# Second stage of a two-MLP kernel: additions and weight conversions held in program order; retention loads and one transpose reordered

## The chip, the cores and the metric

The kernel runs on one core of one Trainium2 chip, as one program. The metric is the device time of an execution in microseconds. The time before is 562.62 us, the median of three runs (562.59 to 562.89). One more execution was profiled; its own time and span are in the table below. Engines are named as the profile names them: PE is TensorE, DVE is VectorE, ACT is ScalarE, POOL is GpSimd, SP is the engine whose queue issues most of the DMAs.

## The reference

Three pieces run one after the other. Retention (linear attention with decay) works on 2 batches of 8 heads, 768 positions and head size 64, here in blocks:

```python
intra = (q_b @ k_b.T * Dmask) @ v_b
inter = (q_b * lam_pow) @ kv_state
out_b = intra + inter
kv_state = lam_block * kv_state + (k_b * rev_pow).T @ v_b
```

Its output, laid out as 1536 tokens by 512, goes through two MLPs of width 2048: `y = relu(x @ w_in)**2 @ w_out`, then `z = leaky(y @ w2_in) @ w2_out` with leaky(h) = max(0.01 h, h). The weights arrive as 64-bit floats. The output is 32-bit.

## The kernel before, in words

**Retention.** The work is cut into 12 units of 128 positions, numbered 0 to 11. Unit i needs its k, q and v (256 KB each, loaded by SP at L65). PE transposes k and q (L279), ACT copies the transposes out of PSUM (L283, L287), PE multiplies them into scores (L300), DVE masks the scores with powers of the decay (L305), PE forms the state update from v and the decayed k (L331) and the output (L360, L362). The loop over i runs one unit ahead in parts: pass i does scores and mask of unit i+1, transposes of unit i+2, then state and output of unit i. Loads run two passes ahead of their use: pass i loads k and q of unit i+4 and v of unit i+2, and pass i+2 uses all three, in the order k, q, v. Three weight pieces are loaded in between. In this part the order on PE and SP is the order of the code.

**The two MLPs.** Each MLP runs in four stages over 512 of the 2048 hidden columns; stage (0, 0) is the first, stage (0, 1) the second. Every matmul is done as three matmuls on operands split into a high and a low part (`three`, L549 to L551). From the second stage on, the first layer treats token tiles 0 and 1 together, as a *pair* (`first_pair`), with seven products of 2 by 2 blocks in place of eight. For each half h = 0, 1 of the stage's columns the products go into four PSUM banks A, B, C, D: A (A11·B11), B (S2·T2), D (A22·T4), B again (S3·T3, added onto the same bank), C (S1·T1), A again (A12·B21), C again (S4·B22). One product is six matmuls of 128x512. Between them DVE makes sums (`plus`, L621), with s1 the copy of A:

- s2 = B + s1, which must have read B before the second B product is added onto it
- r22 = B + s1 with the full B, then s1 = D + r22, which is hidden block 1 of its half for token tile 0
- r22 = C + r22, which must have read C before the second C product is added onto it
- s2 = C + s2 with the full C

`put` sends each finished block through `activate`: in the second stage ACT does relu (L487), the square into the high part (L488, tile g0h or g1h) and the square in place (L489), then DVE subtracts to the low part (L493, tile g0l or g1l). The blocks of token tile 0, h by block, are: block 1 from s1, block 0 from A. The second layer (`second`) starts with g0h and g0l of token tile 0.

**Weight conversion.** Each 64-bit weight piece (tile raw) is turned into float parts by a row of DVE steps (L145, L146, L148, L151 on tile hb) behind one ACT step (L142); for the next stage's pair, sums of weight blocks follow (L446 to L451, tiles rb and sw) and a low part (L169). `convert` issues one such step at each `yield` of PE's work that does not say False. L151 frees the raw tile, so that SP may issue the next weight load.

**What sets the order.** PE, and in retention SP too, run in code order. For DVE, ACT and POOL the tile scheduler chooses the order in each engine's queue from priorities (`plus` and `put` run with a raised priority), except for steps given to `keep_in_program_order`. Once built, each engine works through its queue in order: an instruction that waits holds up all that are behind it.

Of the kernel before, what the change touches and what calls it, by code (L numbers as in the profile page):

```python
# [15 lines left out]
ALU = mybir.AluOpType  # L16
# [4 lines left out]
def tile_retention_then_two_mlps(  # L21
# [39 lines left out]
    def plain():  # L61
        return fp.tile([P, TT], F32, tag="f", name="f")

    def dma(dst, src):
        return nc.sync.dma_start(dst, src)  # L65
# [7 lines left out]
    def source(l, s, n, h):  # L73
        w = ((w1, w2), (w3, w4))[l][n]
        if n == 0:
            return w[:, s * FS + h * CW:s * FS + (h + 1) * CW].rearrange("(k p) f -> p k f", p=P)
        return w[s * FS + h * CW:s * FS + (h + 1) * CW, :].rearrange("(k p) f -> p k f", p=P)

    order = [(0, 0, 0, 0), (0, 0, 0, 1), (0, 0, 1, 0), (0, 0, 1, 1)]
    stages = [(l, s) for l in range(2) for s in range(NS)]  # L80
# [10 lines left out]
    def fetch():  # L91
        if todo:
            key = todo.pop(0)
            r = raw.tile([P, 4 * CW], I64, tag="raw", name="raw")
            k = 4 if key[2] == 0 else 2
            dma(r.rearrange("p (k f) -> p k f", k=k), source(*key))
            fetched.append((key, r))
# [80 lines left out]
    def convert(pin=False):  # L178
        for piece in list(at_work):
            step = next(piece[1], False)  # L180
            if step is False:
                at_work.remove(piece)
            elif step is not None:
                if pin:
                    tc.keep_in_program_order(step)
                return
        if fetched and len(at_work) < 2:
            begin(pin)
# [18 lines left out]
    def retention(ctx_att, att):  # L207
# [10 lines left out]
        def load(i, name):  # L218
            b, c = units[i]
            t = nat[name].tile([P, H, D], F32, tag=name, name=name)  # L220
            dma(t, {"q": q, "k": k, "v": v}[name][b, :, c * C:(c + 1) * C, :].rearrange("h p d -> p h d"))
            nats[i, name] = t

        ve = nc.vector
# [40 lines left out]
        def transposes(i, names="kq"):  # L265
            early = i < 4
            if names[0] == "k":
                both = tr.tile([P, 2, NP, 2, D], F32, tag="kq", name="kqT", bufs=2)
                kT[i], qT[i] = (both[:, n] for n in range(2))
            for name in names:  # L270
                n, dst = ((0, kT), (1, qT))[name == "q"]
                if early:
                    ps = [bank()[:, 0:NP * D].rearrange("p (a s) -> p a s", a=NP) for _ in halves]
                elif n == 0:
                    two = [bank().rearrange("p (n a s) -> p n a s", n=2, a=NP) for _ in halves]
                src = nats[i, name]
                for p in range(NP):
                    for half, r in enumerate(halves):
                        nc.tensor.transpose(ps[half][:, p] if early else two[half][:, n, p],  # L279
                                            src[r, 2 * p:2 * p + 2, :].rearrange("s h d -> s (h d)"), ident[r, r])  # L280
                if early:
                    for half in range(2):
                        nc.scalar.copy(dst[i][:, :, half], ps[half])  # L283
                    dst[i] = dst[i].rearrange("p a f s -> p a (f s)")
            if not early:
                for half in range(2):
                    nc.scalar.copy(both[:, :, :, half], two[half])  # L287
                kT[i], qT[i] = (both[:, n].rearrange("p a f s -> p a (f s)") for n in range(2))
# [81 lines left out]
        n_units = len(units)  # L370
# [15 lines left out]
        mask(0)  # L386
        scale_q(1)
        for i in range(n_units):
            if i + 4 < n_units:
                load(i + 4, "k")  # L390
                load(i + 4, "q")
            if i + 2 < n_units:
                load(i + 2, "v")
            if i == 3:
                next(piece)
            if i == 9:
                next(piece)
                fetch()
                fetch()
            if i + 1 < n_units:  # L400
                scores(i + 1)
                mask(i + 1)
            if i == 1:
                state(i)
                output(i, range(2))
            if i + 2 < n_units:
                transposes(i + 2)
                scale_q(i + 2)
            if i == 1:
                output(i, range(2, NP))  # L410
            else:
                state(i)
                output(i)
            if i + 1 < n_units:
                scale_k(i + 1)
            for _ in range({5: 1, 6: 2, 7: 1, 8: 1, 11: 2}.get(i, 0)):
                convert(pin=True)
# [160 lines left out]
    def first_pair(l, s):  # L578
        last = (l, s) == stages[-1]
        new_g(l, s, 0)  # L580
        new_g(l, s, 1)
        ve = nc.vector
        w = {}
        for h in range(2):
            hi, lo = wts[l, s, 0, h]
            for i in range(2):
                for j in range(2):
                    w[h, f"A{i + 1}{j + 1}"] = [x[:, 2 * j:2 * j + 2, i * P:(i + 1) * P] for x in (hi, lo)]
            for n in range(4):
                w[h, f"S{n + 1}"] = [sums[l, s, 0, h][:, part, n] for part in range(2)]  # L590
        x = {
            "B11": (xhi[0][:, 0:2], xlo[0][:, 0:2]),
            "B21": (xhi[0][:, 2:4], xlo[0][:, 2:4]),
            "B22": (xhi[1][:, 2:4], xlo[1][:, 2:4]),
            "T1": (xhi[1][:, 0:2], xlo[1][:, 0:2]),
        }
        for n in (2, 3, 4):
            x[f"T{n}"] = (tt[n][:, 0], tt[n][:, 1])
        ps, s1, s2, r22 = {}, {}, {}, {}

        def product(h, where, a, b, start=True):
            if start:
                ps[h, where] = bank()
            (ah, al), (bh, bl) = w[h, a], x[b]
            ops = []
            for j in range(2):
                ops += [(ah[:, j], bh[:, j]), (ah[:, j], bl[:, j]), (al[:, j], bh[:, j])]
            three(ps[h, where], ops, start, True, not start)
            return ps[h, where]

        def put(h, src, r, i, t):
            m = 2 * h + i
            with tc.high_priority(offset=400 if t == 0 else 0):
                if last:
                    activate_last(t, m, src)
                else:
                    activate(l, src, r, g[t][0][:, m], g[t][1][:, m], src is r and (l, s) != stages[1])

        def plus(h, out, where, other):
            with tc.high_priority(offset=400):  # L620
                ve.tensor_tensor(out=out, in0=ps[h, where], in1=other, op=ALU.add)  # L621

        both = range(2)
        for h in both:
            b = product(h, "A", "A11", "B11")
            s1[h] = plain()
            nc.scalar.copy(s1[h], b)
            yield True
        for h in both:
            product(h, "B", "S2", "T2")  # L630
            s2[h] = plain()
            plus(h, s2[h], "B", s1[h])
            yield True
        for h in both:
            product(h, "D", "A22", "T4")
            yield (l, s) != stages[1]
        if last:
            opened.add(("sums", l, s))
        for h in both:
            product(h, "B", "S3", "T3", False)  # L640
            r22[h] = plain()
            plus(h, r22[h], "B", s1[h])
            plus(h, s1[h], "D", r22[h])
            put(h, s1[h], s1[h], 1, 0)
            yield last
        for h in both:
            product(h, "C", "S1", "T1")
            plus(h, r22[h], "C", r22[h])
            yield (l, s) != stages[1]
        for h in both:  # L650
            put(h, product(h, "A", "A12", "B21", False), plain(), 0, 0)
            yield last
        for h in both:
            product(h, "C", "S4", "B22", False)
            plus(h, s2[h], "C", s2[h])
            yield last
        for h in both:
            put(h, r22[h], r22[h], 1, 1)
            put(h, s2[h], s2[h], 0, 1)
        if last:  # L660
            sums_last(0)
            sums_last(1)
# [162 lines left out]
    with tc.manual_schedule(engines={mybir.EngineType.PE}):  # L825
        for l, s in stages:
            for part in stage(l, s):
                for room in part:
                    if room is not False:
                        convert()  # L830


# [23 lines left out]
```

## Time and profile before

| what | value |
|---|---|
| time, median of three runs | 562.62 us |
| the profiled execution's own time | 563.24 us |
| its span on the core | 561.5 us |
| PE busy | 551.3 us (98%) |
| DVE busy | 413.5 us (74%) |
| ACT busy | 296.2 us (53%) |
| stretch 0 to 54 us: PE, DMA share | 49.41 us busy, 0.95 |
| stretch 60 to 120 us: PE, DVE | 60.00 us and 59.04 us busy |
| stretch 120 to 160 us: PE, DVE | 37.94 us and 30.37 us busy |

The span is the time between the first and the last instruction on the core; 1.74 us of the execution lie around it. Retention fills the first 54 us. The first stage runs from there to 119.45 us and the second stage's pair starts there. A busy share says only that an engine had something to do; which wait ended last in a place is read from the views of waits and of time order.

### The profile page before, as it was taken

What the parts mean: (1) busy time and instruction counts of PE and PEld (TensorE: products, weight loads), DVE (VectorE), ACT (ScalarE), POOL (GpSimd) and SP (SyncE); (2) the same over time, 40 slices, a digit from 0 to 9 for tenths busy, and PEclk for the clock granted to TensorE, in tenths of its full rate; (3) what the DMA queues carried; (4) which work ended last, traced back from release to release, by engine and by line L of the source; (5) the groups of instructions that cost most, each with busy time, mean ns of one, the idle gap of its engine ahead of it and who ended that gap; (6) DMA issues with size and microseconds to landing.
All of it is one profiled execution on the core that took longest, in us unless ns stands there. A gap on an engine that the chain in (4) does not pass through costs nothing.

```text
span 561.5 us, 8346 instructions
## 1 busy us (share of the span) xinstructions
PE 551.3 (98%) x3245; PEld 465.5 (83%) x3245; DVE 413.5 (74%) x603; ACT 296.2 (53%) x470; POOL 87.6 (16%) x99
## 2 busy tenths in 40 slices
PE   7999999999999999999999999999999999999997
PEld 6989888887788888888888888888888888888897
DVE  5668999999662895639989996549472774629877
ACT  3444898555782456553366576445462375436520
POOL 4855000000203101220000000000213011310131
PEclk9999999999999999999999999999999999999999
DMA  8998255454619516584413233533729423560534
GB/s 201 213 229 264 76 166 190 169 159 141 129 25 245 123 12 142 150 150 138 144 56 114 75 97 128 176 124 109 118 84 182 111 23 52 75 76 1 163 139 149
DMA packets 68055, 71.84 MB, mean 128 GB/s; under 512 B 39856, under 2 KB 43952, under 8 KB 68016
## 3 DMA queue, kind: packets, MB, share of 16 engines
q1 hardware_dynamic: 60960, 58.60, 34.0%
q0 software_dynamic: 6912, 12.59, 15.9%
q8 instruction: 25, 0.41, 0.3%
q10 hardware_dynamic: 144, 0.13, 0.1%
q14 instruction: 14, 0.11, 0.1%
HBM read 49.29 MB, written 22.02 MB: 127 GB/s over the span
## 4 chain that ended last, share of the span: by engine, by line
PE 82%; DVE 8%; DMA 6%; ACT 2%; issue 1%; SPq 0%; ACTq 0%
PE ps L551 75%; DMA raw<-in_moe_w_in 2%; PE ps L300 2%; DMA raw<-in_moe_w_out 2%; PE ps L362 2%; PE ps L360 1%; DVE hb L151 1%; PE ps L331 1%; DMA v<-in_v 1%; ACT hb L142 1%; DVE f L479 1%; PE ps L279 1%; DMA k<-in_k 1%; DVE hb L148 1%; DVE t L69 1%
## 5 line engine op out<-in xcount | busy, mean ns | idle before, releaser
L670 POOL DMA_DIRECT2D spill<-f x48 | 42.6, 893 | 406.1 <-ACT f L666 260.4
L551 PE MATMUL ps<-xhi,w1h 128*128 128x512 f32 x216 | 84.2, 390 | 0.0
L551 PE MATMUL ps<-xlo,w1h 128*128 128x512 f32 x216 | 84.1, 389 | 0.0
L551 PE MATMUL ps<-xhi,w1l 128*128 128x512 f32 x216 | 84.1, 389 | 0.0
L666 ACT COPY f<-ps 128x512 f32<-128x512 f32 x72 | 42.0, 585 | 74.3 <-PE ps L551 74.0
L169 DVE TENSOR_TENSOR w2l<-hb,w2h 128x1024 fp32r<-128x1024 f32 x16 | 19.7, 1229 | 61.2 <-ACT w2h L167 60.9
L621 DVE TENSOR_TENSOR f<-ps,f 128x512 f32<-128x512 f32 x70 | 46.5, 693 | 6.4 <-PE ps L551 6.3
L493 DVE TENSOR_TENSOR g0l<-f,g0h 128x512 fp32r<-128x512 f32 x52 | 35.5, 694 | 21.3 <-ACT f L492 14.7
L551 PEld LDWEIGHTS ps<-xhi,w1l 128*128 128x128 f32 x216 | 40.5, 188 | 8.5
L551 PEld LDWEIGHTS ps<-xhi,w1h 128*128 128x128 f32 x216 | 40.5, 188 | 8.5 <-issue 0.2
L551 PEld LDWEIGHTS ps<-xlo,w1h 128*128 128x128 f32 x216 | 40.5, 188 | 8.4
L551 PE MATMUL ps<-g0l,w2h 128*128 128x512 f32 x112 | 43.8, 391 | 0.8 <-DVE g0l L493 0.8
L551 PE MATMUL ps<-g0h,w2h 128*128 128x512 f32 x112 | 43.6, 389 | 0.0
L551 PE MATMUL ps<-g0h,w2l 128*128 128x512 f32 x112 | 43.6, 389 | 0.0
L151 DVE SCALAR_TENSOR_TENSOR hb<-raw,hb 128x1024 uint16<-128x1024 uint32 x31 | 42.5, 1371 | 0.3
L142 ACT ACTIVATE hb<-raw 128x1024 f32<-128x1024 f32 x31 | 35.5, 1145 | 13.2 <-DMA raw<-in_moe_w_in 6.8
L551 PE MATMUL ps<-t,sw 128*128 128x512 f32 x168 | 40.4, 389 | 0.0
L551 PE MATMUL ps<-w2h,g0l 128*128 128x512 f32 (+1 forms) x104 | 39.6, 381 | 0.0
L551 PE MATMUL ps<-w2l,g0h 128*128 128x512 f32 (+1 forms) x104 | 39.6, 381 | 0.0
L551 PE MATMUL ps<-w2h,g0h 128*128 128x512 f32 (+1 forms) x104 | 39.6, 381 | 0.0
L148 DVE SCALAR_TENSOR_TENSOR hb<-raw,hb 128x1024 uint32<-128x1024 uint32 x31 | 38.0, 1224 | 0.4
L551 PE MATMUL ps<-xhi,sw 128*128 128x512 f32 x112 | 36.9, 390 | 1.3 <-DVE f L621 1.3
(180 smaller groups left out, 1218.7 us busy)
## 6 DMA issues: line engine op xcount, KB each, us to landing
raw<-in_moe_w_out SPq DMA_DIRECT2D x16, 1024.0 KB, 4.9
raw<-in_moe_w_in SPq DMA_DIRECT2D x15, 1024.0 KB, 5.7
spill<-f POOLq DMA_DIRECT2D x48, 256.0 KB, 4.2
spill<-f SPq DMA_DIRECT2D x24, 256.0 KB, 2.4
k<-in_k SPq DMA_DIRECT2D x12, 256.0 KB, 4.6
q<-in_q SPq DMA_DIRECT2D x12, 256.0 KB, 4.6
v<-in_v SPq DMA_DIRECT2D x12, 256.0 KB, 4.6
f<-spill SPq DMA_DIRECT2D x12, 256.0 KB, 2.7
```

The lines of the kernel that those rows point to most:

```text
L69: nc.vector.tensor_tensor(out=lo, in0=src, in1=hi, op=ALU.subtract)
L142: step = nc.scalar.activation(hf, w_hi.bitcast(F32), AF.Abs)
L148: yield ve.scalar_tensor_tensor(out=hb, in0=w_hi, scalar=0xC0000000, in1=hb, op0=ALU.bitwise_and, op1=ALU.bitwise_or)
L151: step = ve.scalar_tensor_tensor(out=half, in0=w_lo, scalar=2.0 ** -29, in1=half, op0=ALU.mult, op1=ALU.add)
L169: yield ve.tensor_tensor(out=lo, in0=hf, in1=hi, op=ALU.subtract)
L300: nc.tensor.matmul(raw_scores[i][par][:, p, :], kT[i][r, p, :], qT[i][r, p, :], start=True, stop=True)
L362: nc.tensor.matmul(ps[r, p, :], vn[:, 2 * p + par, :], Pm[n][:, par, p, :], start=c == 0, stop=True)
L493: nc.vector.tensor_tensor(out=glo, in0=r, in1=ghi, op=ALU.subtract)
L551: nc.tensor.matmul(ps, a, b, start=start and n == 0, stop=stop and n == len(ops) - 1, skip_group_check=again)
L621: ve.tensor_tensor(out=out, in0=ps[h, where], in1=other, op=ALU.add)
L666: nc.scalar.copy(f, src)
L670: nc.gpsimd.dma_start(dst, f, accum_op=ALU.add)
```

## The change

It has two parts. In the second stage alone, the additions of `plus` and the DVE steps of `convert` are held in program order, and three more yields of `first_pair` say False, so that no conversion step is issued at them. In retention, passes 2 and later issue v ahead of k and q, and the transposes of k of unit 2 move ahead of the scores of unit 1.

```diff
         for i in range(n_units):
-            if i + 4 < n_units:
-                load(i + 4, "k")
-                load(i + 4, "q")
-            if i + 2 < n_units:
-                load(i + 2, "v")
+            ahead = [(i + 4, "k"), (i + 4, "q"), (i + 2, "v")]
+            for n, name in ahead if i < 2 else ahead[2:] + ahead[:2]:
+                if n < n_units:
+                    load(n, name)
...
+            if i == 0:
+                transposes(2, "k")
             if i + 1 < n_units:
                 scores(i + 1)
                 mask(i + 1)
...
             if i + 2 < n_units:
-                transposes(i + 2)
+                transposes(i + 2, "kq" if i else "q")
                 scale_q(i + 2)
...
         def plus(h, out, where, other):
             with tc.high_priority(offset=400):
-                ve.tensor_tensor(out=out, in0=ps[h, where], in1=other, op=ALU.add)
+                step = ve.tensor_tensor(out=out, in0=ps[h, where], in1=other, op=ALU.add)
+            if (l, s) == stages[1]:
+                tc.keep_in_program_order(step)
...
             plus(h, s2[h], "B", s1[h])
-            yield True
+            yield (l, s) != stages[1]
...
                 for room in part:
                     if room is not False:
-                        convert()
+                        convert(pin=(l, s) == stages[1])
```

DVE's queue before, in the second stage's pair (buffer numbers kept: ps_1754 is bank C of h = 0, ps_1762 of h = 1; hb_1679 and hb_1829 are two weight pieces of the third stage; f_1689 is s1 of h = 1):

```order
L148 SCALAR_TENSOR_TENSOR hb_1829<-raw_1651,hb_1829 128x1024
L621 TENSOR_TENSOR f_1689<-ps_1721,f_1747 128x512
L493 TENSOR_TENSOR g0l_1667<-f_1677,g0h_1666 128x512
L621 TENSOR_TENSOR f_1734<-ps_1754,f_1734 128x512
L621 TENSOR_TENSOR f_1747<-ps_1762,f_1747 128x512
L446 TENSOR_TENSOR rb_1859<-hb_1679 128x256
L447 TENSOR_TENSOR rb_1859<-hb_1679 128x256
L493 TENSOR_TENSOR g0l_1667<-f_1689,g0h_1666 128x512
L448 TENSOR_TENSOR rb_1859<-rb_1859,hb_1679 128x256
L151 SCALAR_TENSOR_TENSOR hb_1829<-raw_1651,hb_1829 128x1024
L493 TENSOR_TENSOR g0l_1667<-f_1776,g0h_1666 128x512
```

The same place now (ps_1692 and ps_1701 are bank B of h = 0 and 1, ps_1750 and ps_1758 are bank C; f_1772 is block 0 of h = 0, out of bank A):

```order
L146 TENSOR_SCALAR hb_1679<-hb_1679 128x1024
L622 TENSOR_TENSOR f_1699<-ps_1692,f_1677 128x512
L622 TENSOR_TENSOR f_1708<-ps_1701,f_1689 128x512
L622 TENSOR_TENSOR f_1730<-ps_1692,f_1677 128x512
L622 TENSOR_TENSOR f_1677<-ps_1710,f_1730 128x512
L494 TENSOR_TENSOR g0l_1667<-f_1677,g0h_1666 128x512
L622 TENSOR_TENSOR f_1743<-ps_1701,f_1689 128x512
L622 TENSOR_TENSOR f_1689<-ps_1717,f_1743 128x512
L494 TENSOR_TENSOR g0l_1667<-f_1772,g0h_1666 128x512
L494 TENSOR_TENSOR g0l_1667<-f_1689,g0h_1666 128x512
L622 TENSOR_TENSOR f_1730<-ps_1750,f_1730 128x512
L622 TENSOR_TENSOR f_1743<-ps_1758,f_1743 128x512
```

The conversion steps have left the pair (they now stand behind the last g1l); the first s2 addition stands behind L146 in place of ahead of it; and the first reading of bank C (f_1730 from ps_1750) now stands behind three subtractions to g0l where it stood behind one.

ACT's queue now, at the same place (ps_1670 and ps_1682 are bank A of h = 0 and 1):

```order
L488 ACTIVATE f_1677<-f_1677 128x512
L489 ACTIVATE g0h_1666<-f_1677 128x512
L490 ACTIVATE f_1677<-f_1677 128x512
L488 ACTIVATE f_1772<-ps_1670 128x512
L488 ACTIVATE f_1689<-f_1689 128x512
L489 ACTIVATE g0h_1666<-f_1772 128x512
L489 ACTIVATE g0h_1666<-f_1689 128x512
L490 ACTIVATE f_1772<-f_1772 128x512
L490 ACTIVATE f_1689<-f_1689 128x512
L488 ACTIVATE f_1783<-ps_1682 128x512
```

Relu of bank A of h = 0 (f_1772) now stands ahead of relu of f_1689, and the two blocks' squares alternate.

SP's queue before, in passes 4 and 5 of retention (k_544, q_546 are of unit 8, v_548 of unit 6; the next three are of units 9, 9 and 7):

```order
L65 DMA raw_471<-in_moe_w_in 128x4x128
L65 DMA k_544<-in_k 128x8x64
L65 DMA q_546<-in_q 128x8x64
L65 DMA v_548<-in_v 128x8x64
L65 DMA k_619<-in_k 128x8x64
L65 DMA q_621<-in_q 128x8x64
L65 DMA v_623<-in_v 128x8x64
```

And now (v_544 is of unit 6, k_546 and q_548 of unit 8):

```order
L65 DMA raw_471<-in_moe_w_in 128x4x128
L65 DMA v_544<-in_v 128x8x64
L65 DMA k_546<-in_k 128x8x64
L65 DMA q_548<-in_q 128x8x64
L65 DMA v_619<-in_v 128x8x64
L65 DMA k_621<-in_k 128x8x64
L65 DMA q_623<-in_q 128x8x64
```

The places in the queue are the same; within each three, v moved to the first place, k to the second and q to the last.

## Rows read from the trace of the kernel before

**Rows 1.** The page: TensorE's granted clock in 40 slices.

```profile
PEclk9999999999999999999999999999999999999999
```

**Rows 2.** Waits of PE: engine, line, releaser: us in total, times, longest.

```profile
PE ps L551 <- DVE f L621: 1.3, 1, 1.3
...
PE ps L331 <- DMA v<-in_v: 0.9, 1, 0.9
PE ps L551 <- DVE g0l L493: 0.8, 1, 0.8
PE ps L300 <- ACT kqT L283: 0.7, 1, 0.7
```

**Rows 3.** PE in order of time, the pair: start us, us, instruction [idle before].

```profile
127.61 2.88 PE L551 MATMUL ps<-t,sw 128*128 128x512 f32 x12
...
134.19 0.39 PE L551 MATMUL ps<-xhi,w1l 128*128 128x512 f32 x1
...
135.55 0.39 PE L551 MATMUL ps<-xhi,w1l 128*128 128x512 f32 x1
137.19 0.50 PE L551 MATMUL ps<-xhi,sw 128*128 128x512 f32 x1 [1.25 <-DVE f L621]
137.53 0.39 PE L551 MATMUL ps<-xlo,sw 128*128 128x512 f32 x1
...
141.24 0.50 PE L551 MATMUL ps<-g0l,w2h 128*128 128x512 f32 x1 [0.81 <-DVE g0l L493]
```

**Rows 4.** DVE in order of time, the pair.

```profile
125.87 0.69 DVE L145 TENSOR_SCALAR hb<-hb 128x1024 f32<-128x1024 f32 x1
126.47 0.69 DVE L621 TENSOR_TENSOR f<-ps,f 128x512 f32<-128x512 f32 x1
...
136.45 1.29 DVE L621 TENSOR_TENSOR f<-ps,f 128x512 f32<-128x512 f32 x2
```

**Rows 5.** ACT in order of time, the pair.

```profile
133.64 0.63 ACT L487 ACTIVATE f<-f 128x512 f32<-128x512 f32 x1 [2.56 <-DVE f L621]
134.30 0.63 ACT L488 ACTIVATE g0h<-f 128x512 fp32r<-128x512 f32 x1
134.97 0.63 ACT L489 ACTIVATE f<-f 128x512 f32<-128x512 f32 x1
...
137.17 0.58 ACT L487 ACTIVATE f<-ps 128x512 f32<-128x512 f32 x1
...
144.89 2.18 ACT L489 ACTIVATE f<-f 128x512 f32<-128x512 f32 x4
```

**Rows 6.** SP's issue of v of units 6 and 7 in order of time.

```profile
29.04 2.07 SPq L65 DMA_DIRECT2D v<-in_v  x1
...
33.91 0.92 SPq L65 DMA_DIRECT2D v<-in_v  x1
```

**Rows 7.** DMA issues at 27.65 to 29.1 us: tile, count, KB, us to landing.

```profile
v<-in_v SPq DMA_DIRECT2D x1, 256.0 KB, 5.9
```

**Rows 8.** DMA issues at 33.9 to 34 us, likewise.

```profile
v<-in_v SPq DMA_DIRECT2D x1, 256.0 KB, 4.2
```

**Rows 9.** Tile v: landing of its twelve loads.

```profile
DMA to landing us min/median/max: 3.8/4.6/5.9
```

**Rows 10.** PE in order of time, retention: q of unit 8, states of units 6 and 7.

```profile
33.72 0.41 PE L279 MATMUL ps<-delta,q 64*128 64x64 f32 x8
35.06 0.69 PE L331 MATMUL ps<-v,kd 128*64 128x64 f32 x16 [0.93 <-DMA v<-in_v]
...
38.22 0.69 PE L331 MATMUL ps<-v,kd 128*64 128x64 f32 x16
```

**Rows 11.** SP's issues behind the pair, in order of time.

```profile
130.99 10.07 SPq L65 DMA_DIRECT2D raw<-in_moe_w_out  x2
```

**Rows 12.** ACT in order of time, 160 to 162 us.

```profile
160.23 1.12 ACT L142 ACTIVATE hb<-raw 128x1024 f32<-128x1024 f32 x1
```

**Rows 13.** PE in order of time, third stage: first use of the weight sums.

```profile
187.39 2.88 PE L551 MATMUL ps<-t,sw 128*128 128x512 f32 x12
```

## The prediction

> **What bounds the kernel now.** I read the page first, then the waits of PE, then PE, DVE and ACT in order of time around the pair of the second stage, and last PE, SP and the landings in retention. On the page the reader is to see that PE sets the time: it is busy in 98% of the span, and its granted clock is at the upper level, 2.4 GHz, in all slices [rows 1]. So the time changes only where PE waits, or by how long its own work is. The waits of PE are few. Two lie in the second stage's pair, 1.3 us for an addition and 0.8 us for a subtraction to g0l; two lie in retention, 0.9 us for v and 0.7 us for ScalarE's copies of the transposes [rows 2]. The order of time puts them in place: the second C product of h = 0 starts at 137.19 after 1.25 us of idling, and the second matmul of the second layer at 141.24 after 0.81 us [rows 3]. In retention the state of unit 6 starts at 35.06 after 0.93 us [rows 10]. Behind 141.24 PE waits for nothing until the end, so a shift of PE there reaches the end undiminished.
>
> **The pair, step by step.** The change issues no conversion step at three more places and holds the additions in code order. In the built order all conversion steps from L148 of hb_1679 on have left the pair. One would read this as a gain, because nothing but additions and g0l is left on DVE. I went through the new queues with the durations of the rows, and two places get worse.
>
> First place: bank B of h = 0. Before, the s2 addition started at 126.47, right behind L145 at 125.87 [rows 4], and PE's second B products started at 127.61 without a wait [rows 3]. Now L146 stands between. It depends on L145, and a dependent step starts some 0.03 us behind the shown end of the one before (133.64 + 0.63 against 134.30 [rows 5]): L146 at 126.59. Steps that don't depend on each other follow at 0.60 us (two additions in 1.29 us, one being 0.69 us [rows 4]): s2 at 127.19, ending at 127.88. PE starts 0.05 us behind such an end (136.45 + 0.69 against 137.19 [rows 3, 4]), at 127.93 in place of 127.61. That is 0.32 us, and after a wait the second matmul follows after 0.34 us in place of 0.227 (137.19 to 137.53; 134.19 to 135.55 is six matmuls [rows 3]), another 0.11. Together PE is 0.43 us late.
>
> Second place: bank C of h = 0. The second C product must wait until the r22 addition has read the bank. In the new queue that addition stands behind g0l of blocks 0 and 1 of halves 0 and 1 (f_1772 and f_1689), and both need three ScalarE steps. Block 0 of h = 0 comes out of bank A, whose product's last matmul starts at 134.19 [rows 3], now 134.62, and is shown to end 0.39 later, at 135.01. Relu starts at 135.04. ScalarE's steps that don't depend on each other follow at 0.52 us (four in 2.18 us, one being 0.62 [rows 5]): relu of f_1689 at 135.56 (its addition chain, with 0.66 us steps as in rows 5, is ready at about 135.07), squares into g0h at 136.08 and 136.60, squares in place at 137.12 and 137.64, ending at 137.75 and 138.27. DVE subtracts at 137.78 and 138.38; the r22 addition runs from 138.98 to 139.67; PE starts at 139.72. Before it started at 137.19: 2.53 us later.
>
> Against that, the wait at 141.24 goes: g0l of block 0 is then long done. From 139.72 the twelve matmuls of the two C products and the first two of the second layer put the second one at 139.72 + 0.34 + 12 x 0.227 = 142.78. Before it stood at 141.24, to which its own restart of 0.11 us belongs, so 141.35. **The pair costs +1.43 us.** If ScalarE's steps all followed at 0.66 us, the two squares in place would end some 0.6 us later, +2.0; if s2 found no wait at bank B, +1.0. I take 1.43, since its durations are of the same instructions on the same engines.
>
> **The conversions that are moved.** They stand now behind the last g1l. The squares that g1l waits for ended at 147.07 (144.89 + 2.18 [rows 5]); 2.53 us later, the moved steps begin near 149.6. What hides them: the sums that they make are first read by PE at 187.39 [rows 13], 38 us on. Two weight loads that were issued from 130.99 on [rows 11] wait for an L151 among these steps and move to about 150 and a few us later; even at twice the longest landing of v, 5.9 us [rows 9], the first is there near 162, about when ScalarE begins the next conversion (160.23 [rows 12]), and 25 us ahead of 187. Cost: nothing; rival (d) is the cover gone. On SP no other load stands behind them that PE needs sooner, and POOL's queue keeps its order.
>
> **Retention.** The loads keep their places in SP's queue, and within each three v gets the first place and q the last. In pass 6 PE uses k, q and v in the order k, q, v. Before, the last place held v of unit 6: issued at 29.04, landed 5.9 us later at 34.94, used at 35.06 [rows 6, 7, 10]. q, which PE wants at 33.72, 0.41 us ahead of v's use [rows 10], had landed. Now q has the place that landed at 34.94 and v is early. So q's transposes start at 35.06, and the state behind them 0.41 us later at 35.47: **+0.41 us**, the wait of 0.93 us on v goes and one of 1.3 us on q comes. The next three repeats it: v of unit 7 was issued at 33.91, landed after 4.2 us at 38.11, and its use at 38.22 followed at once [rows 6, 8, 10], so q of unit 9 in that place keeps PE 0.41 us late. The moved transposes of k of unit 2 fill a wait of PE, the 0.7 us on ScalarE's copies [rows 2]: a gain of 0.7 us at the most, which q's wait of unit 8 swallows whole. Bounds: if none of these loads held PE, 0.93 and 0.7 us would be won, -1.6; if a place that landed in 4.2 us took 5.9, +2.1. I take +0.41, the value for the landings as the rows show them.
>
> The first stage waits for DVE nowhere on PE, and DVE's work in it is started by PE's results, so a shift of retention goes through to the pair. **Sum:** 1.43 + 0.41 = +1.84 us on the profiled execution's 563.24 us, 565.1. That execution is 0.62 us above the median of the runs, so the median should be 562.62 + 1.84 = 564.5.
>
> **Rivals.** (a) The loads land earlier relative to PE than in the one profile, and retention wins its 1.6 us while the pair loses 1.43: 562.4, no change. For it: landings of v spread from 3.8 to 5.9 us [rows 9], and 29.04 + 3.8 is 32.84, ahead of q's use. Against it: two threes in a row, units 6 and 7, show the last place just in time or late [rows 10]. The Trainium skill ("DMA: Bandwidth & Descriptors", section on queues, rings and completion order) says that completions on one issuing queue need not come in issue order; by that q could overtake its neighbours, and the time would be this rival's. The rows show the last-issued load as the late one. Chance 0.16.
>
> (b) The additions are free as the conversions leave, and the pair's two waits go: -2.06 us, with +0.41 in retention 561.0; with retention's gain 559.0, faster. It decides if the subtractions ahead of the r22 addition are done before bank C is full, for instance because ScalarE is much quicker than in its rows. Against it: bank A's product comes behind bank C's on PE, so g0l of f_1772 cannot be ready by then. Chance 0.08.
>
> (c) PE idles 3.35 us at bank C (136.37 to 139.72), longer than any wait that the trace shows, and its granted clock falls. Each matmul would then take twice its 0.227 us; if it lasted as long as the idling, half of 3.35 us, 1.7 us, is lost: 566.2. The rows show the upper level throughout [rows 1], so nothing here prices it. The Trainium skill ("TensorE: Matmul & The Clock Gate", "What's actually happening") says that an idle TensorE drops to 1.2 GHz and needs activity to come back; no run here shows that yet. Chance 0.07.
>
> (d) The moved conversions come late for the third stage, and PE waits there: some us more, 566 or above. Against it the slack from 162 to 187 us. Chance 0.03.
>
> **How the numbers follow.** My forecast has 0.66, with a range of its own from 563.6 to 565.4 (pair 1.0 to 2.0, retention 0 to 0.8). 0.2% is 1.13 us, about what a measurement here tells from no change; no change is 561.5 to 563.7. Slower: the forecast but for 0.04 at its lower edge, with (c) and (d), 0.72. Same: rival (a) and that edge, 0.20. Faster: (b), 0.08. The range from 562.4 to 565.8 takes in (a) and leaves out (b), (c) and (d).
>
> **What would show it.** The profile after should show: the additions as PE's releaser at bank C with an idle of about 3.3 us and the product starting near 140.1 (with retention's shift); a short wait at bank B, where there was none; no wait for g0l at the second layer; in retention a wait for q of unit 8 of about 1.3 us at the transposes and none for v; nothing new on PE beyond 143 us. I am wrong if the second C product starts before 137.5, if retention's first matmul of the MLP comes before its old time, or if PE waits in the third stage.

## The result, and the profile after

The changed kernel takes 566.03 us (median of 12 runs, 564.42 to 568.98); the kernel before, on the same chips, 563.08 us (12 runs). The ratio is 1.0051, with a 95% interval from 1.0032 to 1.0070: the change makes the kernel slower, by 2.9 us (1.8 to 3.9). Forecast were 564.5 us and 1.84 us more than before. Of the 1.57 us between 566.03 and the unrounded 564.46, 0.46 are in the base (563.08 against the 562.62 of the first three runs) and 1.1 in the change. What follows is about these 1.1 us; they lie in a step that the prediction had down as a rival. The forecast's +1.84 lies on the lower edge of this interval (1.8 to 3.9), so the excess rests on the experiments below more than on this one set.

The profiled execution ended after 565.28 us (span 563.5), 2.04 us behind that of before, so it agrees with the forecast's +1.84. Its waits of TensorE, in the columns of [rows 2]:

```profile
PE ps L552 <- DVE f L622: 3.5, 2, 3.3
...
PE ps L279 <- DMA q<-in_q: 1.2, 2, 0.9
...
PE ps L331 <- DMA v<-in_v: 0.4, 1, 0.4
```

The wait for an addition has grown from 1.3 to 3.3 us, the one for g0l is gone, and q has taken the first place among the loads (v's 0.4 us are near 11 us). TensorE in order of time, as in [rows 3] (the idle time before an instruction in brackets):

```profile
128.53 3.02 PE L552 MATMUL ps<-t,sw 128*128 128x512 f32 x12 [0.17 <-DVE f L622]
...
136.60 0.39 PE L552 MATMUL ps<-xhi,w1l 128*128 128x512 f32 x1
140.32 0.50 PE L552 MATMUL ps<-xhi,sw 128*128 128x512 f32 x1 [3.33 <-DVE f L622]
140.66 0.39 PE L552 MATMUL ps<-xlo,sw 128*128 128x512 f32 x1
...
143.40 0.39 PE L552 MATMUL ps<-g0l,w2h 128*128 128x512 f32 x1
...
143.85 0.39 PE L552 MATMUL ps<-g0h,w2h 128*128 128x512 f32 x1
```

ScalarE and VectorE of the same execution show why 140.32 is so late:

```profile
135.67 0.60 ACT L488 ACTIVATE f<-ps 128x512 f32<-128x512 f32 x1 [1.63 <-PE ps L552]
136.16 0.62 ACT L488 ACTIVATE f<-f 128x512 f32<-128x512 f32 x1
136.68 1.14 ACT L489 ACTIVATE g0h<-f 128x512 fp32r<-128x512 f32 x2
137.72 1.14 ACT L490 ACTIVATE f<-f 128x512 f32<-128x512 f32 x2
```

```profile
127.19 0.69 DVE L146 TENSOR_SCALAR hb<-hb 128x1024 uint32<-128x1024 uint32 x1
127.80 1.28 DVE L622 TENSOR_TENSOR f<-ps,f 128x512 f32<-128x512 f32 x2
...
138.37 1.29 DVE L494 TENSOR_TENSOR g0l<-f,g0h 128x512 fp32r<-128x512 f32 x2 [2.29 <-ACT f L490]
139.58 1.28 DVE L622 TENSOR_TENSOR f<-ps,f 128x512 f32<-128x512 f32 x2
```

VectorE idles 2.29 us, though the addition at 139.58 could run: its bank had been full since about 134.3, but its queue is in order, and two subtractions into g0l stand ahead of it, waiting for ScalarE's squares. TensorE starts at 140.32, when the first addition has read its bank. In retention, against [rows 10]:

```profile
35.11 0.46 PE L279 MATMUL ps<-delta,q 64*128 64x64 f32 x8 [0.95 <-DMA q<-in_q]
35.50 0.69 PE L331 MATMUL ps<-v,kd 128*64 128x64 f32 x16
...
38.63 0.46 PE L279 MATMUL ps<-delta,q 64*128 64x64 f32 x8 [0.23 <-DMA q<-in_q]
39.02 0.69 PE L331 MATMUL ps<-v,kd 128*64 128x64 f32 x16
```

The state of unit 6 is 0.44 us later than before (35.06), that of unit 7 0.80 (38.22); the first matmul of the MLP starts at 54.63, 0.59 us later than before's 54.04.

So this one profile holds the forecast's sum almost term by term, and not the median's 2.9 us. What it does not hold is in the list of the executions: it had a mean granted clock of 0.999, while 10 of the 12 executions had 0.997 or less. The two theories from here on: **waits alone** (TensorE's queue and the durations of the rows give the time, +1.84), and **the clock**, rival (c): behind bank C's wait TensorE's granted clock falls in most executions. A third, that loads in retention land late, was kept beside them.

### The profile page after: what moved, and what is told of

It is laid out like the page before. It is cut to its first block, busy times and chain, and to the rows that moved or that the text cites. A ratio compares the mean times of both kernels' runs of the same rounds, so it can differ in the third digit from the quotient of the medians.

```text
span 563.5 us, 8338 instructions
## 1 busy us (share of the span) xinstructions
PE 552.2 (98%) x3245; PEld 465.9 (83%) x3245; DVE 413.5 (73%) x603; ACT 296.4 (53%) x470; POOL 88.0 (16%) x99
## 4 chain that ended last, share of the span: by engine, by line
PE 83%; DVE 8%; DMA 4%; ACT 2%; SPq 1%; issue 1%; POOL 0%; ACTq 0%; DVEq 0%
PE ps L552 77%; DMA raw<-in_moe_w_out 2%; PE ps L362 2%; PE ps L300 2%; PE ps L360 1%; SPq L65 1%; PE ps L331 1%; DMA raw<-in_moe_w_in 1%; DVE hb L151 1%; DVE f L480 1%; DMA v<-in_v 1%; DMA q<-in_q 1%; ACT hb L142 1%; PE ps L279 1%; DVE t L69 1%
```

## Experiments

Each kernel is compared with the kernel before, timed beside it on the same chip. Ratios carry their 95% intervals.

**The changed kernel once more**, unaltered, for a profile of an execution that the clock did disturb.

> The changed kernel once more, unaltered, for a profile of an execution like those that make its median, and for its time beside the combined kernel's. Clock theory: the profiled execution shows, behind the wait at bank C, matmuls 0.43 us apart at a granted clock of 0.5, and an end 2 to 4 us later than in the profile taken first (565.3 us); of the executions most are at a mean granted clock of 0.997 or less; +2.5 to +3 us against the kernel before. Waits alone: +1.8 to +2.0 us, clock 0.999 or more in most.

Measured: ratio 1.0053 (1.0034 to 1.0072), 567.34 against 564.46 us, 3.0 us above before (1.9 to 4.1); 10 of 12 executions at 0.997 or less; the profiled one ended at 569.7 us. TensorE in it, and its stretches (start and end, length, busy us and instructions of PE, PEld (TensorE's weight loads), DVE, ACT and POOL, then the granted clock, the DMA share and GB/s):

```profile
139.39 0.39 PE L552 MATMUL ps<-xhi,w1l 128*128 128x512 f32 x1
143.11 0.78 PE L552 MATMUL ps<-xhi,sw 128*128 128x512 f32 x1 [3.33 <-DVE f L622]
143.68 0.63 PE L552 MATMUL ps<-xlo,sw 128*128 128x512 f32 x1
144.11 1.06 PE L552 MATMUL ps<-xhi,sw 128*128 128x512 f32 x2
...
147.79 0.40 PE L552 MATMUL ps<-g0l,w2h 128*128 128x512 f32 x1
```

```profile
143.00:144.00 1.00, 0.89 (x2) 0.80 (x3) 1.00 (x3) 1.00 (x3) 0.00 (x0) 0.58 0.00 0
144.00:145.00 1.00, 1.00 (x4) 0.72 (x4) 0.25 (x1) 1.00 (x3) 0.00 (x0) 0.50 0.03 8
...
146.00:146.50 0.50, 0.50 (x3) 0.41 (x2) 0.44 (x1) 0.00 (x0) 0.00 (x0) 0.50 0.00 0
146.50:147.00 0.50, 0.50 (x3) 0.40 (x3) 0.25 (x1) 0.22 (x1) 0.00 (x0) 0.93 0.00 0
```

The same wait of 3.33 us, but behind it the clock is at 0.50, 1.2 GHz, until about 146.6, and matmuls follow 0.43 us apart (143.68 to 144.11) in place of 0.23. From the C product to the second matmul of the second layer it takes 147.79 - 143.11 = 4.68 us; without a fall it was 143.40 - 140.32 = 3.08. The fall costs 1.60 us here. Of the 4.4 us by which this execution is later, 2.6 were there at the first MLP matmul (57.25 against 54.63): waits of 1.49 and 0.41 us for k and q near 35 us, and another fall from 37.3 to 40.8. The last 0.2 us lie at bank B. So a low mean clock does not say where an execution's fall was; only a profile does.

**Only the second stage's part**: the kernel before with the diff's last three places (the held additions, the missing steps, the pinned conversions) and its own retention. The missing steps are two, one behind each half of bank B; the three in the prediction and ahead of it are a miscount, on which no number rests.

> Only the second stage's part of the change; the loads and transposes of retention are as in the kernel before. Waits alone (PE's queue and the durations in the trace): TensorE waits some 3.3 us for the r22 addition at bank C, the second layer's second matmul comes 1.4 to 1.5 us later than before, and the median is 1.5 us above the kernel before, mean granted clock 0.999 to 1.000. Clock theory: in most executions the granted clock falls to its lower level behind that wait of 3.3 us; mean granted clock about 0.996 and median 2.3 to 2.5 us above. Retention theory (the missing microsecond comes from loads that land late): +1.5 us and no fall of the clock.

Measured: ratio 1.0060 (1.0038 to 1.0083), 567.1 against 563.63 us; 3.4 us above before (2.1 to 4.7); all 6 executions at 0.997 or less. The profile has the fall:

```profile
139.00 0.80 PE L551 MATMUL ps<-xhi,sw 128*128 128x512 f32 x1 [3.33 <-DVE f L621]
...
145.42 0.39 PE L551 MATMUL ps<-g0h,w2h 128*128 128x512 f32 x1
```

```profile
138.00:139.00 1.00, 0.00 (x1) 0.00 (x1) 1.00 (x3) 0.94 (x3) 0.00 (x0) 0.70 0.00 0
139.00:140.00 1.00, 1.00 (x2) 0.83 (x3) 1.00 (x2) 1.00 (x3) 0.00 (x0) 0.50 0.00 0
...
145.00:146.00 1.00, 1.00 (x5) 0.78 (x5) 0.81 (x2) 0.75 (x2) 0.00 (x0) 0.88 0.00 0
```

TensorE had no work from 135.7 to 139.0; the clock fell while it idled and came back at about 145.2. From the C product (139.00) to the fourth matmul of the second layer (145.42) it took 6.42 us; in the first profile of the changed kernel the same stretch took 143.85 - 140.32 = 3.53. This fall cost 2.9 us. The interval leaves out the +1.43 us that the prediction gave the pair. So the excess sits in the pair's part, and loads that land late, which this kernel's retention does not change, are not needed for it.

**The wait filled**: the changed kernel, with matmuls that nothing needs in the wait.

```diff
+        if (l, s) == stages[1]:
+            for n in range(13):
+                nc.tensor.matmul(ps[0, "B"], w[0, "A12"][0][:, 0], x["B21"][0][:, 0], start=True, stop=True)
         for h in both:
             product(h, "C", "S4", "B22", False)
```

> The changed kernel with 13 additional matmuls of 128 x 512 (13 x 0.227 us = 2.95 us) into a bank whose content is no longer needed, placed in TensorE's queue just ahead of the second product of bank C: the addition that TensorE waits for comes no earlier, but TensorE works through most of that wait. Waits alone: the second layer starts where it does in the changed kernel, and the median is the changed kernel's, +2.9 us against the kernel before. Clock theory: the mean granted clock is 0.999 to 1.000 and the median is 0.8 to 1.3 us below the changed kernel's, +1.8 to +2.1 us against the kernel before.

Measured: ratio 1.0030 (1.0013 to 1.0046), 1.7 us above before (0.7 to 2.6); 1 of 12 executions at 0.997 or less.

```profile
137.21 3.11 PE L658 MATMUL ps<-xhi,w1h 128*128 128x512 f32 x13
140.71 0.50 PE L552 MATMUL ps<-xhi,sw 128*128 128x512 f32 x1 [0.39 <-DVE f L622]
...
143.83 0.39 PE L552 MATMUL ps<-g0l,w2h 128*128 128x512 f32 x1
```

The addition comes no earlier (the C product starts 140.71 - 54.83 = 85.88 us behind the first MLP matmul; in the changed kernel 140.32 - 54.63 = 85.69), and TensorE does 13 matmuls more; yet the median goes down by 0.2% against the changed kernel's. The two intervals still overlap; what decides is the count: 1 of 12 executions in place of 20 of 24 in the changed kernel's two sets, and of 6 of 6 in the second stage's part alone, which was timed in the same set as the filled kernel. With the fall taken away, what is left is +1.7 us: the forecast's 1.84 lies well within its interval.

**Half filled**: the same with 6 matmuls.

> The changed kernel with 6 additional matmuls (6 x 0.227 us = 1.36 us) where the filled kernel had 13, so that TensorE's wait at bank C is some 2.0 us in place of 3.3. The addition waited for comes at the same time. Waits alone: the median is the changed kernel's and the filled kernel's in equal measure. Clock theory, with the length of the idling deciding how often the clock falls: executions with a mean granted clock of 0.997 or less become fewer than in the changed kernel (10 of 12) and more than in the filled one (1 of 12), and the median lies between theirs, +1.7 to +2.9 us against the kernel before. If any idling at that place were enough: as in the changed kernel, +2.9 us.

Measured: ratio 1.0024 (1.0007 to 1.0040), 1.4 us above before; 3 of 11 executions at 0.997 or less. The profile is one of these:

```profile
137.52 1.52 PE L658 MATMUL ps<-xhi,w1h 128*128 128x512 f32 x6
141.02 0.72 PE L552 MATMUL ps<-xhi,sw 128*128 128x512 f32 x1 [1.98 <-DVE f L622]
...
145.69 0.39 PE L552 MATMUL ps<-g0l,w2h 128*128 128x512 f32 x1
```

A wait of 1.98 us can still be followed by a fall (141.02 to 145.69 is 4.67 us, 1.6 more than without one). The time can't be told from the filled kernel's, so the forecast of a median between the two was not met. The count lies between theirs, but 3 of 11 can't be told from the 13 of 80 of the kernel before either.

**The subtractions held too**: the changed kernel, with the pair's four g0l of the second stage put behind bank C's additions in the same program order.

```diff
+        def rest():
+            return nc.vector.tensor_tensor(out=glo, in0=r, in1=ghi, op=ALU.subtract)
+
+        if held is None:
+            rest()
+        else:
+            held.append(rest)
...
+        for n in (0, 2, 1, 3) if held else ():
+            with tc.high_priority(offset=400):
+                step = held[n]()
+            tc.keep_in_program_order(step)
```

> The changed kernel, but the second stage's four subtractions into g0l are also held in program order, behind the additions of bank C. Waits alone: the wait of 3.3 us at bank C goes, and with it what the kernel before waited there and at the second layer (2.06 us); bank B's 0.4 us and retention's 0.5 us stay: some 1.1 us below the kernel before. Clock theory: the same, with a mean granted clock near 1.000 in all executions, so some 4 us below the changed kernel's median. If something else than these subtractions holds bank C's addition: +2 to +3 us as in the changed kernel.

Measured: 562.13 us, ratio 0.9970 (0.9957 to 0.9983), 1.7 us below before (1.0 to 2.4); no execution at 0.997 or less. VectorE and TensorE of it:

```profile
129.99 3.43 DVE L630 TENSOR_TENSOR f<-ps,f 128x512 f32<-128x512 f32 x5 [1.15 <-PE ps L558]
134.09 0.69 DVE L630 TENSOR_TENSOR f<-ps,f 128x512 f32<-128x512 f32 x1 [0.67 <-PE ps L558]
...
138.80 1.29 DVE L495 TENSOR_TENSOR g0l<-f,g0h 128x512 fp32r<-128x512 f32 x2 [3.42 <-ACT f L490]
```

```profile
136.39 0.39 PE L558 MATMUL ps<-xhi,w1l 128*128 128x512 f32 x1
136.61 0.39 PE L558 MATMUL ps<-xhi,sw 128*128 128x512 f32 x1
...
139.56 0.48 PE L558 MATMUL ps<-g0l,w2h 128*128 128x512 f32 x1
```

Both additions of bank C have run by 134.8, TensorE goes on at 136.61 without a wait, and VectorE's 3.42 us of idling ahead of g0l hold nobody. One edit turns the change from slower to faster: those subtractions were what held bank C.

**Retention's part, whole and in halves**, each on the kernel before.

> Only the retention part of the change (v ahead of k and q, transposes of k of unit 2 moved); the second stage is as in the kernel before. Waits alone: the first MLP matmul comes 0.4 to 0.6 us later, median +0.4 to +0.6 us, mean granted clock as in the kernel before. Clock theory (the fall belongs to bank C's wait): the same +0.5 us, clock near 1.000. Retention theory: +1.3 to +1.5 us, with waits for q between 33 and 39 us that differ from one execution to the next.

> The kernel before with only the order of the loads changed from unit 2 on (v of two units on ahead of k and q of four units on). Forecast's step: waits for q near 33 and 38 us take the place of the wait for v, +0.4 us. Rival from the trace of the retention part alone (waits for k too, 0.96 us and 0.18 us, beside 0.34 and 0.29 us for q): +0.8 to +1.2 us. Rival that landings differ more from one execution to the next than between the two orders: no change, 0 +- 0.3 us.

> The kernel before with only the transposes of k of unit 2 moved ahead of the scores of unit 1. Waits theory: the 0.7 us that TensorE waits there for ScalarE's copies shrinks to about 0.4 us, as it did in the traces of the changed kernel, and nothing else moves: median 0.3 us below the kernel before. Rival (the loads decide when retention ends, whatever is gained early): no change within 0.2 us, with a wait for v or k near 35 us that is longer by what was gained.

Measured: both edits 1.0008 (0.9995 to 1.0022), +0.45 us; the loads' order alone 0.9998 (0.9985 to 1.0011); the moved transposes alone 0.9980 (0.9967 to 0.9994), 1.1 us faster (0.3 to 1.9), where 0.3 us were expected. Its one profile does not show where that would come from: the wait for ScalarE's copies is gone, but a wait of 0.77 us for v has come near 11 us, and the first MLP matmul starts at 54.23, no earlier than before's 54.04. The intervals of the first two hold both 0 and the forecast's +0.41. The start of the first MLP matmul in the profiles says why it can't be told: with the loads as before it lies between 53.02 and 56.00 (five profiles), with v ahead between 54.23 and 57.25 (seven); the two upper ends, 56.00 and 57.25, have a fall of the clock in retention. Without these two, the means are 54.05 (four) and 54.93 (six): that points the forecast's way, but executions of one order still differ by 1.3 us and more. The rival that landings differ more than the orders is not refuted.

**Versions for use.** The first keeps the kernel before's retention, holds the subtractions as above, and takes the step ahead of bank B's additions out; the second adds the moved transposes.

```diff
             nc.scalar.copy(s1[h], b)
-            yield True
+            yield h == 0 or (l, s) != stages[1]
```

> Retention as in the kernel before; in the second stage the conversions leave, additions and the four subtractions into g0l are held in program order with the additions of bank C ahead of the subtractions, and the conversion step ahead of bank B's additions leaves as well. Waits theory: TensorE waits nowhere between 125 and 145 us; the kernel before's 1.25 + 0.81 us go: 2.0 us below the kernel before, and with no fall of the clock (some 3 of 29 executions of the kernel before had one) a little more in the mean. Rival: a wait for g0l of block 2 or 1 comes in the second layer, since ScalarE's order puts steps for the other tile between: 1.0 to 1.5 us below.

> The best pair (conversions out, subtractions held behind bank C's additions, bank B clear) with the loads of retention as in the kernel before and only the transposes of k of unit 2 moved. If the two gains add up: 0.46% for the pair and 0.2% for the transposes, 2.6 + 1.1 = 3.7 us below the kernel before; from the waits alone 2.06 + 0.3 = 2.4 us. If the loads hold retention's end whatever is gained early, and the transposes' gain was chance: as the best pair alone, 2.0 to 2.6 us.

Measured: 562.34 us, ratio 0.9954 (0.9938 to 0.9971), and 561.94 us, ratio 0.9972 (0.9947 to 0.9997). Both are faster than before, by 2.6 and 1.6 us; between the two, and against the kernel with held subtractions, the intervals overlap, so it stays open what the transposes add. In the profiles TensorE has no wait in the pair (0.02 us idle from 125 to 145 us in the first, none from 125 to 141 in the second), as the second one's stretches show:

```profile
133.00:137.00 4.00, 4.00 (x19) 3.32 (x18) 1.74 (x3) 3.97 (x9) 0.00 (x0) 1.00 0.00 0
137.00:141.00 4.00, 4.00 (x19) 2.98 (x17) 1.85 (x3) 4.00 (x9) 0.00 (x0) 1.00 0.01 2
```

2 of 6 and 4 of 12 executions were still at 0.997 or less. The profile of the first one has such a fall, not in the pair but in retention, behind a wait of 1.21 us for k:

```profile
7.15 0.46 PE L279 MATMUL ps<-delta,k 64*128 64x64 f32 x8 [1.21 <-DMA k<-in_k]
...
7.64 2.00 PE L300 MATMUL ps<-kqT 64*128 64x128 f32 x15
```

```profile
7.00:8.00 1.00, 0.85 (x15) 0.85 (x17) 0.90 (x3) 0.35 (x2) 0.01 (x1) 0.98 1.00 228
8.00:9.00 1.00, 1.00 (x11) 1.00 (x12) 0.00 (x0) 0.30 (x2) 1.00 (x1) 0.50 0.93 212
...
14.00:15.00 1.00, 1.00 (x22) 1.00 (x22) 0.32 (x1) 0.72 (x3) 0.00 (x0) 0.60 1.13 255
```

## Why the prediction was wrong, step by step

The executions with a mean granted clock of 0.997 or less, by the wait at bank C:

| kernels | wait at bank C | such executions |
|---|---|---|
| changed (two sets), second stage's part alone | 3.3 us | 26 of 30 |
| half filled | 2.0 us | 3 of 11 |
| retention's part, whole and in halves | 1.2 to 1.4 us | 6 of 34 |
| before (three sets) | 1.25 us | 13 of 80 |
| filled | 0.4 us | 1 of 12 |
| held subtractions, and the two versions for use | none | 6 of 30 |

The count takes in falls in retention too, which can come whatever the wait at bank C is (the first version for use shows one), so a rate near that of the kernel before need not belong to bank C.

1. **The failed step is rival (c), which the prediction set against its sum at a chance of 0.07 because [rows 1] show the upper level throughout.** "PE idles 3.35 us at bank C ... and its granted clock falls" is what happens in most executions, and the sum has no term for it. Its price was about right: 1.7 us were forecast, from a fall as long as the idling; 1.6 us in the changed kernel, 1.6 in the half-filled and 2.9 in the second stage's part alone were measured. The first two falls lasted about as long as the wait of 3.33 us, the third twice as long. That the rival's 566.2 us stands so near the median's 566.03 is in part chance: it counts from 562.62, and 0.46 us of the median are the base's. What failed is the reading: [rows 1] come from one execution with no wait of that length, so they say nothing about one. The Trainium skill ("TensorE: Matmul & The Clock Gate", "What's actually happening") has the rule that an idle TensorE drops to 1.2 GHz; the granted clock of 0.50 behind this wait agrees with it, and in the first profile the clock stayed at 1.00 behind the same wait.
2. **The sum without the clock holds.** Bank B: +0.43 forecast; in the first profile 128.53 - 127.61 - 0.59 (retention) = 0.33, and 0.11 at the restart. Bank C: 139.72 forecast, 140.32 measured, which is 139.73 without retention's 0.59. The wait at 141.24 is gone. The second matmul of the second layer: 143.40 - 54.63 = 88.77 us behind the MLP's first matmul; before 141.35 - 54.04 = 87.31; +1.46 against +1.43. With the clock kept up by filler the whole change measures +1.7 against 1.84. The changed kernel's own executions without a fall bound it loosely: two in each set, 1.8 us above before's median in the first and 0.2 in the second.
3. **The cause at bank C holds**: with the two subtractions behind the addition the wait is gone and the time is below that of before.
4. **The moved conversions cost nothing**, as said: behind the pair no profile with the moved conversions has a wait of TensorE.
5. **Retention is open in size.** The mechanism, a wait for q in place of v's, is in the profiles (0.44 us at unit 6 against 0.41), but the times bound it only to -0.3 to +1.2 us. The prediction's list of waits in retention left out one for k near 6.9 us (1.00 us in the profile before, 0.23 in the first profile after); such waits differ from one profile to the next, so part of the agreement in the first profile is luck.
6. **The range's upper end, 565.8, left (c) out**; it would have had to reach to 566.2, a case that had its own worked price.

Rival (a) failed: the pair's loss was not made up. Rival (b) failed as argued, g0l was not ready. Rival (d), a wait in the third stage, is in no profile.

## What to carry to other kernels

When a change makes a longer wait than any that the trace shows, the trace is silent on what TensorE's clock does behind it: add the price of a fall to the wait's own, and give it a real chance. When steps are held in program order, hold those between them as well, or place them by when their inputs are ready: an in-order queue stops for the one step that was left to the scheduler. A wait that can't be removed can be filled with matmuls that nothing needs; here the median came out 0.2% lower, with intervals that overlap.

## What the hardware showed unexpectedly

A fall does not come every time: with the same wait of 3.33 us the first profile shows a clock of 1.00 right through, the repeated one 0.50. It lasts longer or shorter (from about 143.2 to 146.6 in one, 138.4 to 145.2 in another), so its cost varies by 1.3 us.

Falls also come behind shorter waits in retention, where TensorE's matmuls are small: behind 1.21 us for k, above, the clock is down from about 8.0 to 14.8 us. There too a fall does not come every time: behind 1.19 us for k the profile of retention's whole part has none. In the kernel before, 13 of 80 executions have a mean of 0.997 or less; none of them was profiled, so where their falls lie is not known.

In the first 11 us TensorE's pace differs between executions even where the granted clock reads 1.00, as it does in both from 7 to 11 us: the 15 matmuls of the first scores took 2.12 us in the profile with held subtractions and 1.26 us in the one with the second stage's part alone.

```profile
7.57 2.12 PE L300 MATMUL ps<-kqT 64*128 64x128 f32 x15
```

```profile
7.36 1.26 PE L300 MATMUL ps<-kqT 64*128 64x128 f32 x15
```
